# Three real products for four in the 128-point complex stages of a spectral and MLP kernel

## The chip, the cores and the metric

The kernel runs on one core of a Trainium2 chip. The metric is the device time of one execution in microseconds (us). Before the change it is 1355.37 us, the median of three runs (1354.95 to 1356.36).

The engines are named as in the profile: PE is TensorE, with PEld its weight loads; DVE is VectorE, ACT is ScalarE, POOL is GpSimd, SP is SyncE.

## The reference

A gated sum of two branches, and its gradients for eight of the inputs:

```python
def A(x, w_r, w_i):                      # spectral branch, x is (1, 2048, 1024)
    X = rfft2(x.astype(float32))
    return irfft2(X * (w_r + 1j * w_i), s=(S, D)).astype(bfloat16)

def B(x, w1, b1, w2, b2):                # MLP branch, F = 3584
    h = x @ w1 + b1
    return relu(h) ** 2 @ w2 + b2

g = sigmoid((x * gate_w).sum(-1, keepdims=True))
out = g * A(x, w_r, w_i) + (1 - g) * B(B_x, w1, b1, w2, b2)
# outputs: out, and the gradients with respect to x, w_r, w_i, w1, b1, w2, b2 and gate_w for grad_out
```

The kernel takes the second transform of 2048 points in the S direction as 16 x 128. The 16-point part and the part along D are done in an earlier stage. What is left for each of 16 residues k is a complex 128-point transform with twiddles, that is a product with a 128x128 complex matrix, cos and sin of which lie in `amat` (forward) and `apmat` (inverse). It is done for two transforms T: the input x (T = 0) and the gradient (T = 1).

## The kernel before

The large products of the MLP (forward, gradients of w1 and w2, gradient of x) are six groups of 896 matmuls of 128x512 in bf16. The spectral work is woven between them: the generator `spectra` is advanced at a fixed rate while `mlp_grads` yields. The program's builder then orders the instructions of each engine.

The stages of this study are in `fft_mid`, which runs beside the gradients of w2 and w1. One step m handles the two residues `pair(m)`, so that m goes from 0 to 7, and j = 0, 1 are the two residues of a pair:

```python
        for m in range(S2 // 2):
            z, am, ap, w = nxt
            if m + 1 < S2 // 2:
                nxt = inputs(m + 1)                      # loads for the next step
            xs = []
            for T in range(2):
                xs.append(spectrum(fb, T, m, z[:, T], am))   # forward, below
                yield
            real_columns(fb, m, z, am, xs, sgn)          # columns l = 0 and 512: tiny matmuls sp
            ...
            for T in range(2):                           # y = X * w, or X * conj(w)
                ...
                V(out=t1_[:, :, :, 0:W1], in0=X, in1=wr, op=ALU.mult)
                V(out=t2_[:, :, :, 0:W1], in0=X, in1=wi, op=ALU.mult)
                V(out=y[:, T, :, 0, 0:W1], ...)
                V(out=y[:, T, :, 1, 0:W1], ...)
                yield
            back(fb, m, y, ap)                           # inverse, below
            yield
            ...                                          # gradients of w: t1_, t2_, gs on VectorE
            nc.scalar.mul(out=gw[:, :, :, 0:W1], in_=gs[:, :, :, 0:W1], mul=GS)
            ...
            yield
```

The forward stage. `V` is a VectorE `tensor_tensor`, `mm` a matmul. A `px` tile is two PSUM banks, real and imaginary part, 512 columns each; there are two such tiles (`ps2`), which `pv` uses too:

```python
    def spectrum(fb, T, m, z, mats):
        if m:
            pm = fb.tile([P, 4, 4, P], FDT, name="pm", tag="pm")
            R, I = zg(z[:, 0]), zg(z[:, 1])[:, ::-1]
            V(out=pm[:, 2:0:-1], in0=R, in1=I, op=ALU.add)
            V(out=pm[:, 0::3], in0=R, in1=I, op=ALU.subtract)
            main = [(pm[:, 0], pm[:, 1]), (pm[:, 2], pm[:, 3])]
        else:
            ...
        x = fb.tile([P, 2, 2, LW], FDT, name=f"x{T}", tag=f"x{T}")
        for j in range(2):
            re, im = main[j]
            C, Sn, N = (mats[:, j, a, :] for a in range(3))      # cos, sin, -sin
            px = fps.tile([P, 2, H], FP32, name="px", tag="ps2", bufs=2)
            mm(px[:, 0, :], lhsT=C, rhs=re, start=True, stop=False)
            mm(px[:, 1, :], lhsT=C, rhs=im, start=True, stop=False)
            mm(px[:, 0, :], lhsT=Sn, rhs=im, start=False, stop=True)
            mm(px[:, 1, :], lhsT=N, rhs=re, start=False, stop=True)
            (nc.scalar.copy if j == 0 else nc.vector.tensor_copy)(
                out=x[:, j, :, 0:H].rearrange("p c (i g) -> p c i g", g=4), in_=px[:].rearrange("p c (g i) -> p c i g", g=4)
            )
        return x
```

The inverse stage `back` does the same four matmuls for `pv[:, 0]` and `pv[:, 1]` out of `y`, with `apmat`, for both T and both j, and copies `pv` to the fp16 tile `v` (ScalarE for j = 0, VectorE for j = 1). Then VectorE forms `pc` out of `v`, and GpSimd issues its store.

Another pair of PSUM buffers, one bank each (tag `tr`), serves the tiny products `sp` and `si` of the two single columns, the transposes and the column sums `prow`. The small inputs of `sp` and `si` are formed on GpSimd (`ed`, `e`).

Of the kernel before, what the change touches and what calls it, by code (L numbers as in the profile page):

```python
# [10 lines left out]
P = 128  # L11
BF16 = mybir.dt.bfloat16
FP16 = mybir.dt.float16
FP32 = mybir.dt.float32
# [3 lines left out]
FDT = FP16  # L18
# [25 lines left out]
def build_consts(g: Geo):  # L44


    S, D, S2 = g.S, g.D, g.S2
    tp = 2.0 * np.pi
    Q = D // 4
    c = {}  # L50
    c["identb"] = np.eye(P, dtype=np.float32).astype(ml_dtypes.bfloat16)
    q = np.arange(P)
    t, pl = q // 8, q % 8
    same = (pl[:, None] == pl[None, :]).astype(np.float64)

    cc = np.arange(16)
    k2 = np.where(cc <= 8, cc, cc - 8)
    ang = tp * ((np.arange(16)[:, None] * k2[None, :]) % 16) / 16
    kf = np.where(cc[None, :] <= 8, np.cos(ang), -np.sin(ang))
    c["kf"] = (kf[t][:, t] * same).astype(FDT_NP)  # L60
    ki = np.where(cc[None, :] <= 8, np.cos(ang), np.sin(ang)).T
    c["ki"] = (ki[t][:, t] * same).astype(FDT_NP)

    w = lambda l, d: tp * ((l[None, :] * d[:, None]) % D) / D
    l4, l42 = np.arange(0, D // 2 + 1, 4), np.arange(2, D // 2, 4)
    lo = np.concatenate([np.arange(1, D // 2, 4), np.arange(3, D // 2, 4)])
    d0, d1 = np.arange(P), np.arange(P, 2 * P)
    dz, dh = d0.copy(), d0.copy()
    dz[0], dh[0] = Q, P
    blk_n = np.concatenate([np.zeros((P, P + 1)), -np.sin(w(l4[1:-1], d0))], axis=1)  # L70
    blk_n[0, : P + 1] = np.cos(w(l4, np.array([P])))[0]
    parts = [
        blk_n, np.cos(w(l4, d0)), np.cos(w(l42, d0)), -np.sin(w(l42, dh)),
        np.cos(w(lo, d0)), np.cos(w(lo, d1)), -np.sin(w(lo, dz)), -np.sin(w(lo, d1)),
    ]
    c["cf"] = np.concatenate(parts, axis=1).astype(FDT_NP)

    v = lambda l, d: tp * ((l[:, None] * d[None, :]) % D) / D
    cof = lambda l: np.where((l == 0) | (l == 2 * Q), 1.0, 2.0)[:, None]
    dq = np.arange(Q)  # L80
    dzq = dq.copy()
    dzq[0] = Q
    m4, m42 = np.arange(0, D // 2, 4), np.arange(2, D // 2, 4)
    m1, m3 = np.arange(1, D // 2, 4), np.arange(3, D // 2, 4)
    da = np.arange(P + 1)
    ev = np.concatenate([np.zeros((P, P + 1)), -2.0 * np.sin(v(m4, da[1:-1]))], axis=1)
    ev[0] = 0.0
    ev[0, : P + 1] = np.cos(np.pi * da)
    parts = [
        ev, cof(m4) * np.cos(v(m4, da)), 2.0 * np.cos(v(m42, d0)), -2.0 * np.sin(v(m42, dh)),  # L90
        2.0 * np.cos(v(m1, dq)), 2.0 * np.cos(v(m3, dq)), -2.0 * np.sin(v(m1, dzq)), -2.0 * np.sin(v(m3, dzq)),
    ]
    c["ci"] = np.concatenate(parts, axis=1).astype(FDT_NP)

    pp = np.arange(P)
    A = np.zeros((P, S2, 3, P))
    B = np.zeros((P, S2, 3, P))
    for k in range(S2):
        th = tp * ((pp[:, None] * (k + S2 * pp[None, :])) % S) / S
        A[:, k, 0, :], A[:, k, 1, :], A[:, k, 2, :] = np.cos(th), np.sin(th), -np.sin(th)  # L100
        th = th.T
        B[:, k, 0, :], B[:, k, 1, :], B[:, k, 2, :] = np.cos(th), np.sin(th), -np.sin(th)
    c["amat"] = (A * XS).astype(FDT_NP)
    c["apmat"] = B.astype(FDT_NP)
    sg = np.ones((P, 2, 2, 2))
    sg[:, 1, 1, :] = -1.0
    c["sgn"] = sg.astype(np.float32)
    return c
# [19 lines left out]
def kernel(  # L128
# [172 lines left out]
    def zg(ap):  # L301
        return ap.rearrange("p (g c i) -> p c g i", g=4, c=2)
# [6 lines that stand above are left out]
            V(out=pm[:, 2:0:-1], in0=R, in1=I, op=ALU.add)  # L309
            V(out=pm[:, 0::3], in0=R, in1=I, op=ALU.subtract)  # L310
            main = [(pm[:, 0], pm[:, 1]), (pm[:, 2], pm[:, 3])]
        else:
            main = [(zg(z[:, j])[:, 0], zg(z[:, j])[:, 1]) for j in range(2)]
        x = fb.tile([P, 2, 2, LW], FDT, name=f"x{T}", tag=f"x{T}")
        for j in range(2):
            re, im = main[j]
            C, Sn, N = (mats[:, j, a, :] for a in range(3))
            px = fps.tile([P, 2, H], FP32, name="px", tag="ps2", bufs=2)
            mm(px[:, 0, :], lhsT=C, rhs=re, start=True, stop=False)
            mm(px[:, 1, :], lhsT=C, rhs=im, start=True, stop=False)  # L320
            mm(px[:, 0, :], lhsT=Sn, rhs=im, start=False, stop=True)
            mm(px[:, 1, :], lhsT=N, rhs=re, start=False, stop=True)  # L322
            (nc.scalar.copy if j == 0 else nc.vector.tensor_copy)(  # L323
                out=x[:, j, :, 0:H].rearrange("p c (i g) -> p c i g", g=4), in_=px[:].rearrange("p c (g i) -> p c i g", g=4)
            )
        return x

    def real_columns(fb, m, z, mats, xs, sgn):

        ed = fb.tile([P, 2, 2, 2, 2], FDT, name="ed", tag="ed", bufs=2)  # L330
        zc = z[:].rearrange("p t c l -> p c t l")[:, :, :, 0 : P + 1 : P]
        G = nc.gpsimd
        sp = tps.tile([P, 2, 2, 4], FP32, name="sp", tag="tr", bufs=2)
        if m:

            G.tensor_copy(out=ed[:, 0], in_=zc)
            G.tensor_copy(out=ed[:, 1, 0], in_=zc[:, 1])
            G.tensor_scalar(out=ed[:, 1, 1], in0=zc[:, 0], scalar1=-1.0, scalar2=None, op0=ALU.mult)
            src = [[ed[:, a].rearrange("p c t l -> p (c t l)") for a in range(2)]] * 2
        else:  # L340

            ed0 = fb.tile([P, 2, 3, 4], FDT, name="ed0", tag="ed0")
            G.memset(ed0[:], 0.0)
            G.tensor_copy(out=ed0[:, :, 0, :].rearrange("p j (t l) -> p j t l", t=2), in_=zc)
            G.tensor_scalar(
                out=ed0[:, :, 2, :].rearrange("p j (t l) -> p j t l", t=2), in0=zc, scalar1=-1.0, scalar2=None, op0=ALU.mult
            )
            src = [[ed0[:, j, a : a + 2, :].rearrange("p a b -> p (a b)") for a in range(2)] for j in range(2)]
        for j in range(2):
            C, Sn, N = (mats[:, j, a, :] for a in range(3))  # L350
            o = sp[:, j].rearrange("p c b -> p (c b)")
            mm(o, lhsT=C, rhs=src[j][0], start=True, stop=False, skip_group_check=True)
            mm(o, lhsT=(Sn if j == 0 else N), rhs=src[j][1], start=False, stop=True, skip_group_check=True)
        for T in range(2):
            V(out=xs[T][:, :, :, 0::H], in0=sp[:, :, :, 2 * T : 2 * T + 2], in1=sgn[:], op=ALU.mult)

    def back(fb, m, ys, mats):

        vs = []
        for T in range(2):  # L360
            y = ys[:, T]
            v = fb.tile([P, 2, 2, LW], FDT, name="v", tag="v", bufs=2)
            for j in range(2):
                C, Sn, N = (mats[:, j, a, :] for a in range(3))
                yr, yi = y[:, j, 0, :], y[:, j, 1, :]
                pv = fps.tile([P, 2, H], FP32, name="pv", tag="ps2", bufs=2)
                mm(pv[:, 0, :], lhsT=C, rhs=yr[:, 0:H], start=True, stop=False)
                mm(pv[:, 1, :], lhsT=C, rhs=yi[:, 0:H], start=True, stop=False)
                mm(pv[:, 1, :], lhsT=Sn, rhs=yr[:, 0:H], start=False, stop=True)
                mm(pv[:, 0, :], lhsT=N, rhs=yi[:, 0:H], start=False, stop=True)  # L370
                (nc.scalar.copy if j == 0 else nc.vector.tensor_copy)(out=v[:, j, :, 0:H], in_=pv[:])
            vs.append(v)

        G = nc.gpsimd
        e = fb.tile([P, 2, 2, 2], FDT, name="e1", tag="e1", bufs=2)
        yl = ys[:, :, :, :, H].rearrange("p t j c -> p j c t")
        G.tensor_scalar(out=e[:, :, 0, :], in0=yl[:, :, 1, :], scalar1=-1.0, scalar2=None, op0=ALU.mult)
        G.tensor_copy(out=e[:, :, 1, :], in_=yl[:, :, 0, :])
        sp = tps.tile([P, 2, 2, 2], FP32, name="si", tag="tr", bufs=2)
        for j in range(2):  # L380
            mm(sp[:, j], lhsT=mats[:, j, 0, :], rhs=yl[:, j], start=True, stop=False, skip_group_check=True)
            mm(sp[:, j], lhsT=mats[:, j, 1, :], rhs=e[:, j], start=False, stop=True, skip_group_check=True)
        for T in range(2):
            v = vs[T]
            nc.vector.tensor_copy(out=v[:, :, :, H], in_=sp[:, :, :, T])
# [663 lines left out]
```

## Time and profile before

| | |
|---|---|
| device time, median of 3 runs | 1355.37 us |
| span of the profiled execution | 1352.3 us |
| granted TensorE clock | 1.00 |
| first forward matmul `px` / last inverse matmul `pv` starts at | 478.7 / 809.5 us |
| `px` matmuls of 128x512 | 128 |
| `pv` matmuls of 128x512 | 128 |
| copies `x` out of `px`: ScalarE / VectorE | 16 / 16 |
| copies `v` out of `pv`: ScalarE / VectorE | 16 / 16 |

How to read it: the page gives for each engine its busy time, share of the span and count of instructions; then the span in 40 slices; then the chain of work that ended last, followed back from the end; then the groups of instructions, with the line, the engine, the operation, what is written and read, shapes and count, and after the bar the busy time in us and the mean of one in ns, and after a second bar the engine's idle time just before them and what ended it. Matmuls are pipelined, and their records overlap: how often one is issued is read from the starts in order of time. Some matmul records are missing from a trace.

### The profile page before, as it was taken

The page shows a single profiled execution, that of the slowest core. Times are in us where ns is not written, and L with a number is a line of the kernel's source. Part 1 is how long each engine was busy: PE and PEld are TensorE (multiplying, and loading weights), DVE is VectorE, ACT ScalarE, POOL GpSimd, SP SyncE. Part 2 cuts the span into 40 slices and gives each one's busy share as a digit, 9 for nine tenths or more (in the row PEclk, how much of TensorE's full clock was granted, in tenths as well). Part 3 has the DMA queues.
Part 4 walks back from the last instruction along what each step waited for, and adds up shares of the span by engine and source line. Part 5 has one row for each costly group of instructions (what it writes and reads, how often), then busy time and mean ns, then how long its engine had stood idle before and what let it go on. Part 6 is the DMA issues. An engine that isn't in the chain of part 4 may idle for free. (4 is left out here: it accounts for less than half of the span.)

```text
span 1352.3 us, 18733 instructions
## 1 busy us (share of the span) xinstructions
PE 1325.9 (98%) x7036; PEld 643.2 (48%) x7146; DVE 750.2 (55%) x1477; ACT 415.2 (31%) x626; POOL 293.2 (22%) x468
## 2 busy tenths in 40 slices
PE   7999999999999999999999999999999999999998
PEld 5654444444444444444444444555545444444443
DVE  7966667666565673556444552323855675642222
ACT  6854555555433313223132233343212100000000
POOL 0222223222322243443332221211101000000000
PEclk9999999999999999999999999999999999999999
DMA  8558778786778978889686448766888764653530
GB/s 284 184 179 252 254 232 258 246 251 225 228 234 242 287 220 194 219 196 235 183 186 190 113 139 245 237 225 215 234 227 232 180 195 132 190 168 94 155 101 24
DMA packets 217092, 273.31 MB, mean 202 GB/s; under 512 B 16988, under 2 KB 152170, under 8 KB 217002
## 3 DMA queue, kind: packets, MB, share of 16 engines
q1 hardware_dynamic: 181306, 153.84, 42.9%
q0 software_dynamic: 35696, 118.27, 27.3%
q8 instruction: 56, 0.92, 0.3%
q14 instruction: 34, 0.28, 0.1%
HBM read 147.25 MB, written 118.51 MB: 197 GB/s over the span
## 5 line engine op out<-in xcount | busy, mean ns | idle before, releaser
L602 PE MATMUL ph<-xT,w1g 128*128 128x512 bf16 x866 | 214.0, 381 | 4.0 <-ACT rT L604 1.7
L612 PE MATMUL pd<-dbT,w2T 128*128 128x512 bf16 x879 | 210.6, 379 | 2.6 <-DVE w2T L634 0.7
L823 PE MATMUL pw<-grd,res 128*128 128x512 bf16 x896 | 200.2, 379 | 0.0
L889 PE MATMUL acc<-w,hblk 128*128 128x512 bf16 x873 | 196.1, 379 | 2.7 <-DVE bGo L891 1.5
L806 PE MATMUL pw<-dbn,grp 128*128 128x512 bf16 x874 | 195.6, 379 | 0.8
L931 PE MATMUL accg<-w1Tr,hblk 128*128 128x512 bf16 x878 | 192.8, 379 | 0.9
L931 PEld LDWEIGHTS <-hblk 128*128 128x128 bf16 x896 | 87.6, 98 | 106.3 <-issue 0.9
L612 PEld LDWEIGHTS <-w2T 128*128 128x128 bf16 x896 | 87.2, 98 | 104.7 <-issue 1.5
L806 PEld LDWEIGHTS <-grp 128*128 128x128 bf16 x896 | 86.9, 98 | 104.2 <-issue 0.9
L889 PEld LDWEIGHTS <-hblk 128*128 128x128 bf16 x896 | 87.0, 98 | 101.1 <-issue 1.7
L602 PEld LDWEIGHTS <-w1g 128*128 128x128 bf16 x896 | 86.8, 98 | 100.0 <-issue 2.8
L823 PEld LDWEIGHTS <-res 128*128 128x128 bf16 x896 | 86.7, 98 | 98.7
L604 ACT ACTIVATE rT<-ph,b1col 128x512 bf16<-128x512 f32 x112 | 77.0, 688 | 144.9 <-PE ph L602 135.2
L616 DVE SCALAR_TENSOR_TENSOR dhT<-pd,rT 128x512 bf16<-128x512 f32 x112 | 75.2, 671 | 65.9 <-PE pd L612 57.3
L810 ACT CAST wo<-pw 128x512 bf16<-128x512 f32 x56 | 32.8, 586 | 161.1 <-PE pw L806 125.1
L936 DVE TENSOR_TENSOR gxo<-accg,g 128x512 bf16<-128x512 f32 x32 | 22.1, 691 | 107.9 <-PE accg L931 102.0
L721 DVE STREAM_TRANSPOSE stg<-h2T 128x512 int32<-128x512 int32 x56 | 39.8, 711 | 73.7 <-ACT h2T L605 73.7
L323 DVE CAST x<-px 128x1024 f16<-128x1024 f32 x16 | 19.6, 1224 | 105.1 <-PE px L322 105.1
L828 ACT CAST wo<-pw 128x512 bf16<-128x512 f32 x56 | 32.9, 587 | 132.0 <-PE pw L823 125.7
L818 POOL DMA_DIRECT2D out_dram<-wo x112 | 56.6, 518 | 72.6 <-ACT wo L810 65.0
L605 ACT ACTIVATE h2T<-rT 128x512 bf16<-128x512 bf16 x112 | 70.6, 630 | 3.1
L728 DVE STREAM_TRANSPOSE stgd<-dhT 128x1024 bf16<-128x1024 bf16 x56 | 69.3, 1239 | 1.3
(175 smaller groups left out, 1423.8 us busy)
## 6 DMA issues: line engine op xcount, KB each, us to landing
h2T_scr<-h2T POOLq DMA_DIRECT2D x28, 512.0 KB, 4.6
h_scr<-stg POOLq DMA_DIRECT2D x28, 512.0 KB, 6.9
dhT_scr<-dhT POOLq DMA_DIRECT2D x28, 512.0 KB, 7.7
dh_scr<-stgd POOLq DMA_DIRECT2D x28, 512.0 KB, 6.6
grp<-h_scr SPq DMA_DIRECT2D x112, 128.0 KB
grd<-dh_scr SPq DMA_DIRECT2D x112, 128.0 KB
hblk<-h2T_scr SPq DMA_DIRECT2D x8, 1792.0 KB
hblk<-dhT_scr SPq DMA_DIRECT2D x8, 1792.0 KB
```

Source lines behind the costliest of these rows:

```text
L602: mm(ph[:], lhsT=w1g[:, dc, fc % 2 * P : (fc % 2 + 1) * P], rhs=xT[:, dc, ss], start=(dc == 0), stop=(dc == DC - 1))
L604: nc.scalar.activation(rT[:], ph[:], ACT.Relu, bias=b1col[:, fc : fc + 1])
L605: nc.scalar.activation(h2T, rT[:], ACT.Square)
L612: mm(pd[:], lhsT=w_[:, ec // 2, ec % 2 :: 2], rhs=dbT[:, ec, ss], start=(ec == 0), stop=(ec == DC - 1),)
L616: return STT(out=dhT, in0=pd[:], scalar=2.0, in1=rT[:], op0=ALU.mult, op1=ALU.mult, accum_out=gb1part[:, fc, sb : sb + 1],)
L721: nc.vector.transpose(out=stg[:, :, c, :], in_=h2T[:, c, :].bitcast(I32).rearrange("p (b i) -> p b i", i=32))
L728: nc.vector.transpose(out=stg[:, :, :, c, :].rearrange("p b k i -> p k b i"), in_=dhT[:, c, :].rearrange("p (k b i) -> p k b i", b=4, i=32),)
L806: mm(pw[:], lhsT=cur[:, t // 2, 2 * fb_ * P + t % 2 : 2 * (fb_ + 1) * P : 2], rhs=dbn[:, t, hf * H : (hf + 1) * H], start=(t == 0), stop=( ...
L818: st(out=dst[q], in_=wo[32 * q : 32 * (q + 1), :])
L823: mm(pw[:], lhsT=xr[t][:, d_ * P : (d_ + 1) * P], rhs=cur[:, t], start=(t == 0), stop=(t == NT - 1),)
L889: mm(acc[:], lhsT=cur[:, fc, t2::2], rhs=w2[:, fc, cs], start=(fc == 0), stop=(fc == FC - 1))
L931: mm(acc[:], lhsT=cur[:, fc, t2::2], rhs=w1T[:, fc, 2 * hf : 2 * hf + 2, :], start=(fc == 0), stop=(fc == FC - 1),)
```

## The change

A complex product (C, S) with (re, im) needs the real part C·re + S·im and the imaginary part C·im - S·re, four real matrix products. They can be had from three: with the common product k = C·(re + im), the real part is k + (S - C)·im and the imaginary part is k - (C + S)·re. The matrices S - C and -C - S are constants and take the places of S and -S in `amat` and `apmat`. The sum re + im is one VectorE addition. The common product belongs to both parts, so it goes to a PSUM tile of its own, is copied to SBUF by ScalarE, and is added to the two others by VectorE as they are moved from PSUM. The change is there to do fewer matmuls.

```diff
@@ build_consts
-        A[:, k, 0, :], A[:, k, 1, :], A[:, k, 2, :] = np.cos(th), np.sin(th), -np.sin(th)
+        A[:, k, 0, :], A[:, k, 1, :], A[:, k, 2, :] = np.cos(th), np.sin(th) - np.cos(th), -np.cos(th) - np.sin(th)
... (B, for apmat, likewise)
@@ spectrum
+            re_, im_ = pm[:, 0::2], pm[:, 1::2]
...
+        sums = fb.tile([P, 2, 4, P], FDT, name="sums", tag="sums", bufs=2)
+        V(out=sums[:], in0=re_, in1=im_, op=ALU.add)
...
-            C, Sn, N = (mats[:, j, a, :] for a in range(3))
             px = fps.tile([P, 2, H], FP32, name="px", tag="ps2", bufs=2)
-            mm(px[:, 0, :], lhsT=C, rhs=re, start=True, stop=False)
-            mm(px[:, 1, :], lhsT=C, rhs=im, start=True, stop=False)
-            mm(px[:, 0, :], lhsT=Sn, rhs=im, start=False, stop=True)
-            mm(px[:, 1, :], lhsT=N, rhs=re, start=False, stop=True)
-            (nc.scalar.copy if j == 0 else nc.vector.tensor_copy)(
-                out=x[:, j, :, 0:H].rearrange("p c (i g) -> p c i g", g=4), in_=px[:].rearrange("p c (g i) -> p c i g", g=4)
+            ps = tps.tile([P, H], FP32, name="pxs", tag="tr", bufs=2)
+            mm(px[:, 0, :], lhsT=mats[:, j, 1, :], rhs=im, start=True, stop=True)
+            mm(px[:, 1, :], lhsT=mats[:, j, 2, :], rhs=re, start=True, stop=True)
+            mm(ps[:], lhsT=mats[:, j, 0, :], rhs=sums[:, j], start=True, stop=True)
+            common = fb.tile([P, H], FP32, name="common", tag="common", bufs=2)
+            nc.scalar.copy(out=common[:], in_=ps[:])
+            by_l = lambda ap: ap.rearrange("p c (g i) -> p c i g", g=4)
+            V(
+                out=x[:, j, :, 0:H].rearrange("p c (i g) -> p c i g", g=4), in0=by_l(px[:]),
+                in1=by_l(common[:].rearrange("p (o l) -> p o l", o=1)).to_broadcast([P, 2, P, 4]), op=ALU.add,
             )
@@ back
+            sums = fb.tile([P, 2, H], FDT, name="ysums", tag="sums", bufs=2)
+            V(out=sums[:], in0=y[:, :, 0, 0:H], in1=y[:, :, 1, 0:H], op=ALU.add)
             for j in range(2):
... (two matmuls to pv, one to pvs in a "tr" buffer, ScalarE copy to common, as above)
+                V(
+                    out=v[:, j, :, 0:H], in0=pv[:],
+                    in1=common[:].rearrange("p (o l) -> p o l", o=1).to_broadcast([P, 2, H]), op=ALU.add,
+                )
@@ real_columns, for m > 0
-            G.tensor_copy(out=ed[:, 0], in_=zc)
+            G.tensor_tensor(out=ed[:, 0, 0], in0=zc[:, 0], in1=zc[:, 1], op=ALU.add)
+            G.tensor_tensor(out=ed[:, 0, 1], in0=zc[:, 1], in1=zc[:, 0], op=ALU.subtract)
@@ back, single columns
+        G.tensor_tensor(out=e[:, :, 1], in0=e[:, :, 0], in1=yl, op=ALU.add)
```

The single columns use the same matrices, so their small inputs on GpSimd are formed anew: since S·b = (S - C)·b + C·b, what multiplied C gets the other operand added. The numbers of their matmuls stay as they were.

More of the change, by code (lines that the diff above doesn't have):

```diff
@@ L99, in build_consts @@
         th = tp * ((pp[:, None] * (k + S2 * pp[None, :])) % S) / S
-        A[:, k, 0, :], A[:, k, 1, :], A[:, k, 2, :] = np.cos(th), np.sin(th), -np.sin(th)
+        A[:, k, 0, :], A[:, k, 1, :], A[:, k, 2, :] = np.cos(th), np.sin(th) - np.cos(th), -np.cos(th) - np.sin(th)
         th = th.T
-        B[:, k, 0, :], B[:, k, 1, :], B[:, k, 2, :] = np.cos(th), np.sin(th), -np.sin(th)
+        B[:, k, 0, :], B[:, k, 1, :], B[:, k, 2, :] = np.cos(th), np.sin(th) - np.cos(th), -np.cos(th) - np.sin(th)
     c["amat"] = (A * XS).astype(FDT_NP)
@@ L311, in spectrum @@
             main = [(pm[:, 0], pm[:, 1]), (pm[:, 2], pm[:, 3])]
+            re_, im_ = pm[:, 0::2], pm[:, 1::2]
         else:
             main = [(zg(z[:, j])[:, 0], zg(z[:, j])[:, 1]) for j in range(2)]
+            re_, im_ = (z.rearrange("p j (g c i) -> p c j g i", g=4, c=2)[:, c] for c in range(2))
+        sums = fb.tile([P, 2, 4, P], FDT, name="sums", tag="sums", bufs=2)
+        V(out=sums[:], in0=re_, in1=im_, op=ALU.add)
         x = fb.tile([P, 2, 2, LW], FDT, name=f"x{T}", tag=f"x{T}")
@@ L340, in real_columns @@
         else:
-            ed0 = fb.tile([P, 2, 3, 4], FDT, name="ed0", tag="ed0")
+            ed0 = fb.tile([P, 2, 4, 4], FDT, name="ed0", tag="ed0")
             G.memset(ed0[:], 0.0)
             G.tensor_copy(out=ed0[:, :, 0, :].rearrange("p j (t l) -> p j t l", t=2), in_=zc)
[L345 to L348, printed above, removed]
+            for a in (1, 3):
+                G.tensor_scalar(
+                    out=ed0[:, :, a, :].rearrange("p j (t l) -> p j t l", t=2), in0=zc, scalar1=-1.0, scalar2=None, op0=ALU.mult
+                )
+            src = [[ed0[:, j, a : a + 2, :].rearrange("p a b -> p (a b)") for a in (0, 2)] for j in range(2)]
         for j in range(2):
-            C, Sn, N = (mats[:, j, a, :] for a in range(3))
             o = sp[:, j].rearrange("p c b -> p (c b)")
-            mm(o, lhsT=C, rhs=src[j][0], start=True, stop=False, skip_group_check=True)
-            mm(o, lhsT=(Sn if j == 0 else N), rhs=src[j][1], start=False, stop=True, skip_group_check=True)
+            mm(o, lhsT=mats[:, j, 0, :], rhs=src[j][0], start=True, stop=False, skip_group_check=True)
+            mm(o, lhsT=mats[:, j, 1 + j, :], rhs=src[j][1], start=False, stop=True, skip_group_check=True)
         for T in range(2):
@@ L362, in back @@
             v = fb.tile([P, 2, 2, LW], FDT, name="v", tag="v", bufs=2)
+            sums = fb.tile([P, 2, H], FDT, name="ysums", tag="sums", bufs=2)
+            V(out=sums[:], in0=y[:, :, 0, 0:H], in1=y[:, :, 1, 0:H], op=ALU.add)
             for j in range(2):
-                C, Sn, N = (mats[:, j, a, :] for a in range(3))
-                yr, yi = y[:, j, 0, :], y[:, j, 1, :]
                 pv = fps.tile([P, 2, H], FP32, name="pv", tag="ps2", bufs=2)
-                mm(pv[:, 0, :], lhsT=C, rhs=yr[:, 0:H], start=True, stop=False)
@@ L368, in back @@
[L368 to L371, printed above, removed]
+                ps = tps.tile([P, H], FP32, name="pvs", tag="tr", bufs=2)
+                mm(pv[:, 0, :], lhsT=mats[:, j, 2, :], rhs=y[:, j, 1, 0:H], start=True, stop=True)
@@ new lines, in back @@
+                mm(pv[:, 1, :], lhsT=mats[:, j, 1, :], rhs=y[:, j, 0, 0:H], start=True, stop=True)
+                mm(ps[:], lhsT=mats[:, j, 0, :], rhs=sums[:, j, :], start=True, stop=True)
+                common = fb.tile([P, H], FP32, name="common", tag="common", bufs=2)
+                nc.scalar.copy(out=common[:], in_=ps[:])
+                V(
+                    out=v[:, j, :, 0:H], in0=pv[:],
+                    in1=common[:].rearrange("p (o l) -> p o l", o=1).to_broadcast([P, 2, H]), op=ALU.add,
+                )
@@ L372, in back @@
             vs.append(v)
         G = nc.gpsimd
-        e = fb.tile([P, 2, 2, 2], FDT, name="e1", tag="e1", bufs=2)
+        e = fb.tile([P, 2, 2, 2, 2], FDT, name="e1", tag="e1", bufs=2)
         yl = ys[:, :, :, :, H].rearrange("p t j c -> p j c t")
-        G.tensor_scalar(out=e[:, :, 0, :], in0=yl[:, :, 1, :], scalar1=-1.0, scalar2=None, op0=ALU.mult)
-        G.tensor_copy(out=e[:, :, 1, :], in_=yl[:, :, 0, :])
+        G.tensor_scalar(out=e[:, :, 0, 0, :], in0=yl[:, :, 1, :], scalar1=-1.0, scalar2=None, op0=ALU.mult)
@@ L379, in back @@
+        G.tensor_copy(out=e[:, :, 0, 1, :], in_=yl[:, :, 0, :])
+        G.tensor_tensor(out=e[:, :, 1], in0=e[:, :, 0], in1=yl, op=ALU.add)
         sp = tps.tile([P, 2, 2, 2], FP32, name="si", tag="tr", bufs=2)
         for j in range(2):
-            mm(sp[:, j], lhsT=mats[:, j, 0, :], rhs=yl[:, j], start=True, stop=False, skip_group_check=True)
-            mm(sp[:, j], lhsT=mats[:, j, 1, :], rhs=e[:, j], start=False, stop=True, skip_group_check=True)
+            mm(sp[:, j], lhsT=mats[:, j, 0, :], rhs=e[:, j, 1], start=True, stop=False, skip_group_check=True)
+            mm(sp[:, j], lhsT=mats[:, j, 1, :], rhs=e[:, j, 0], start=False, stop=True, skip_group_check=True)
```

## The prediction

> **What bounds the kernel now.** I read the page from the top: busy shares, chain, groups; then the busy time by stretches, and last the order of time on each engine around one of the changed stages.
>
> The first part of the page and the chain (part 4):
>
> ```profile
> PE 1325.9 (98%) x7036; PEld 643.2 (48%) x7146; DVE 750.2 (55%) x1477; ACT 415.2 (31%) x626; POOL 293.2 (22%) x468
> ...
> PE 22%; issue 0%; DVE 0%
> ```
>
> TensorE is busy 98% of the span, and the chain that ended last holds TensorE alone, as far back as it could be followed. So a matmul that goes away should shorten the run, unless TensorE then waits.
>
> The busy time by stretches; the columns are the stretch, its length, the busy time and count of each engine, the granted clock, the DMA share:
>
> ```profile
> 478.00:815.00 337.00, 335.49 (x1588) 152.28 (x1607) 178.44 (x266) 93.90 (x120) 116.03 (x206) 1.00 0.75 187
> 815.00:1352.00 537.00, 527.19 (x2718) 252.77 (x2756) 247.16 (x578) 79.78 (x93) 51.23 (x93) 1.00 0.62 178
> ```
>
> All changed stages lie in the first of the two (their first matmul starts at 478.7 us, their last at 809). There TensorE idles 337.0 - 335.5 = 1.5 us, VectorE is busy 53% and ScalarE 28%. Nothing there waits on TensorE's account now; I ask what will.
>
> The groups, kept apart by shape (mean ns of one after the bar):
>
> ```profile
> L367 PE MATMUL pv<-y,apmat 128*128 128x512 f16 x32 | 12.1, 378 | 0.7 <-DVE v L371 0.2
> L371 DVE CAST v<-pv 128x1024 f16<-128x1024 f32 x16 | 19.6, 1222 | 9.0 <-PE pv L370 9.0
> L371 ACT CAST v<-pv 128x1024 f16<-128x1024 f32 x16 | 16.1, 1009 | 5.9 <-PE pv L370 5.9
> L388 DVE TENSOR_TENSOR pc<-v 128x1024 f16<-128x1024 f16 x14 | 9.7, 690 | 3.3 <-ACT v L371 2.9
> L936 DVE TENSOR_TENSOR gxo<-accg,g 128x512 bf16<-128x512 f32 x32 | 22.1, 691 | 107.9 <-PE accg L931 102.0
> L810 ACT CAST wo<-pw 128x512 bf16<-128x512 f32 x56 | 32.8, 586 | 161.1 <-PE pw L806 125.1
> ```
>
> These are my price list. Last, TensorE, VectorE and ScalarE in order of time round the inverse stage of m = 2 (start, duration):
>
> ```profile
> 581.96 0.17 PE L352 MATMUL sp<-ed,amat 128*128 128x8 f16 x1
> ...
> 592.42 0.38 PE L367 MATMUL pv<-y,apmat 128*128 128x512 f16 x1
> 592.64 0.38 PE L368 MATMUL pv<-y,apmat 128*128 128x512 f16 x1
> ```
> ```profile
> 582.53 1.23 DVE L432 TENSOR_TENSOR t<-x,w 128x2052 f16<-128x2052 f16 x1
> ...
> 592.98 0.69 DVE L447 TENSOR_TENSOR gs<-t 128x1026 f16<-128x1026 f16 x1
> 594.36 1.23 DVE L371 CAST v<-pv 128x1024 f16<-128x1024 f32 x1 [0.69 <-PE pv L370]
> ```
> ```profile
> 592.67 0.59 ACT L810 CAST wo<-pw 128x512 bf16<-128x512 f32 x1 [2.91 <-PE pw L806]
> 593.70 1.92 ACT L449 ACTIVATE gw<-gs 128x2052 bf16<-128x2052 f16 x1 [0.45 <-DVE gs L447]
> ```
>
> Two things: a matmul is issued every 0.216 us although its record lasts 0.38; and VectorE works without a pause from the `sp` matmul to the end of `gs`, at 593.67, which is 1.25 us after `pv` has begun. The slack of VectorE at this point is already used up.
>
> [...] So a removed matmul is worth 0.216 us and not 0.378. [...] 1024 elements take 1222 ns from PSUM and 690 ns from fp16 SBUF. [...]
>
> **The change, part by part.**
>
> *Removed from TensorE.* There are 8 steps m, 2 transforms T, 2 blocks j, forward and inverse: 64 blocks, each with three matmuls of 128x512 in place of four. 64 x 0.216 = 13.8 us. The tiny matmuls (`sp`, `si`) stay 32 of each kind.
>
> *VectorE.* Before: 32 casts of 1024 from PSUM at 1.22 (the other 32 are ScalarE's). After: 64 adds of 1024 with one PSUM and one fp32 operand. L936 is that form at 512 elements, 691 ns, against 690 ns for 1024 in fp16[...]. Added: 32 x 1.22 = 39 us. Then 32 sums of 1024 in fp16 at 0.69 = 22 us. Together 61 us in this stretch: 178 + 61 = 239 of about 330, 73%. VectorE doesn't become the bound by throughput.
>
> *ScalarE.* Away: 32 x 1.01 = 32 us. Added: 64 casts of 512 at 0.586 = 37.5 us. Even.
>
> *GpSimd.* One small addition more for `ed` and one for `e1` in each step, 0.2 to 1.2 us each going by the small copies at L337, L377. `e` is ready some 1.0 us before `pv` begins in the trace (590.15 + 1.25 = 591.4), and its matmul comes later than before; hidden.
>
> *New latency.* A `px`/`pv` buffer used to come free one cast (1.0 or 1.2 us, on two engines side by side) after its last matmul. Now: third matmul, ScalarE copy 0.59, then VectorE add 1.22, and all adds on one engine. There are still two such buffers, and two for the common product.
>
> I laid the order of instructions of the built program, engine by engine, against these durations. In the inverse stage TensorE issues: two `pv` matmuls and one common for T0 j0, the same for j1 (6), one filler of the large product, common of T1 j0, two fillers, common of T1 j1, one filler, then `pv` of T1 j0. So `pv` of T1 j0 is reached after 12 x 0.216 = 2.59 us and needs the add of T0 j0 done.
>
> - Steps with 48 fillers between `sp` and `pv`, which are m = 1, 2, 3, 7. The built order puts the two `ysums` (0.61 each from issue to issue, and a short wait: 1.3) and the `gs` group ahead of the first add. `gs` ends at 1.25 + 1.3 = 2.55 after `pv` begins. The add of T0 j0 then runs 2.6 to 3.85. Stall: 3.87 - 2.59 = 1.28 us. The second add ends at 4.97; TensorE reaches its buffer at 3.87 + 0.43 + 4 x 0.216 = 5.16, no wait. 4 x 1.28 = 5.1 us.
> - m = 0 has the other small matmuls between and another order: about 0.4 us.
> - m = 4, 5, 6 have 64 fillers: `gs` is done before `pv`, the add waits only for the copy (0.9 to 1.5 us), runs to 2.7: 0.15 us each, 0.45.
> - Forward stages: mostly 32 fillers (6.9 us) lie between T0 and T1, and VectorE's chain there (pm 0.68, two adds 1.15 each, pm, sums) is done in about 5.7 us. Only m = 3 has 16 (3.5 us): 0.5 us. There ScalarE also stood behind an output store before (its copy of `px` came 3 us late); as it now feeds VectorE, that may cost 2 to 3 us. I put 1.7 for m = 3 in all.
>
> Stalls: 5.1 + 0.4 + 0.45 + 1.7 = 7.7 us. Net: 13.8 - 7.7 = 6.1 us. 1355.4 - 6.1 = 1349.3 us. Nothing after this stretch changes on TensorE, so the gain should reach the end.
>
> **The rivals.**
>
> *All hidden.* The fillers cover every eviction and the whole 13.8 us arrive: 1341.6. For it: the 1.5 us of idle now, 73% VectorE load, fillers placed around the waits. Against it: VectorE has no pause before `pv` at m = 2, and it gets 1.3 us more there.
>
> *VectorE's chain sets the pace.* An early delay isn't made up within a step, so that `sums` of the next forward stage is late too, stalls at the forward and the inverse stages sum to the saving or more: 1355 to 1362. For it: [...] `gw` (1.92 us on ScalarE, waiting for `gs`) stands between the commons of T0 and T1 in m = 1, 2, 3, 7. Against it: VectorE idles some 8.6 us per step before the first `px` cast and 6.2 before the second, and the added work is 7.7 us per step, so each step should catch up.
>
> *A buffer shared with others.* The common products use the two PSUM buffers that `sp`, `si` and `prow` use. If a late copy held these, TensorE would wait at `si` or `sp`: perhaps 0.5 us a step, 4 us in all, 1353. The built order puts `si` late, which speaks against much of it.
>
> **Range and chances.** No stall gives 1341.6, my sum 1349.3, twice my stalls 1357. The low side is held by TensorE's arithmetic. I take 1343 to 1356. Faster by over 2% would need under 1328.3, twice the matmul time removed: 0.01. Slower by over 2%, above 1382.5, would need 40 us of stalls, 5 a step: 0.02. Within 2%: 0.97.
>
> **What would show each step.** The added time on VectorE: 64 adds near 1.22 us, 32 sums near 0.69. TensorE's busy count down by 64 matmuls; its idle time in the stretch up from 1.5 to about 9 us, put down to the VectorE add at the `pv` matmul of T1, 1.3 us each in m = 1, 2, 3, 7 and next to nothing in m = 4, 5, 6. The stretch from first `px` to last `pv` shorter by about 6 us, the time before and after unchanged. I am wrong if the adds take longer than 1.3 us because of their strided output or the broadcast operand (then every stall grows by the difference), if the waits at `px` exceed those at `pv`, or if the stretch behind it moves by more than 2 us.

## The result, and the profile after

The changed kernel takes 1352.74 us (median of 4 runs, 1350.59 to 1353.24) against 1355.16 us for the kernel before on the same chip: a ratio of 0.9979 (0.9961 to 0.9996). The gain is 2.4 us where 6.1 was predicted. A second measurement, ten runs, is among the experiments below: 1351.38 us, 0.9977 (0.9968 to 0.9986). The experiments ran on three chips (1 to 4, 5 to 8 and 9 to 11), each beside the kernel before, with medians of 1354.46, 1354.68 and 1354.87 us; a ratio is to the kernel before on the same chip.

From the page of the changed kernel, first the busy shares, then the chain that ended last:

```profile
PE 1322.1 (98%) x7082; PEld 637.1 (47%) x7082; DVE 824.3 (61%) x1541; ACT 418.4 (31%) x658; POOL 299.3 (22%) x484
...
PE 20%; DMA 1%; DVE 1%; SPq 0%; issue 0%; DVEq 0%
PE accg L946 14%; PE acc L904 6%; DMA go<-in_grad_out_dram 1%; DVE af L898 0%; PE prow L762 0%; DVE ot L905 0%; DVE junk L906 0%; DVE junk L894 0%; SPq L914 0%; DVE gxo L951 0%; SPq L861 0%; DVE ev L496 0%; DVE ev L498 0%; DVE ev L499 0%; DVE ev L500 0%
```

Before, this chain was TensorE alone. Now a load (`go`, the output gradient) and some VectorE work on it stand in it, in the MLP's output stage (`acc`, the last group of matmuls but one), which the change doesn't touch.

The busy time by stretches (stretch, length, busy time and count of PE, PEld, DVE, ACT, POOL, granted clock, DMA share, GB/s); the first again runs from the first `px` to past the last `pv`:

```profile
478.00:812.00 334.00, 324.99 (x1546) 145.52 (x1545) 253.16 (x330) 97.24 (x153) 122.47 (x222) 1.00 0.75 188
812.00:1351.00 539.00, 530.54 (x2756) 253.03 (x2754) 246.39 (x578) 79.74 (x93) 51.22 (x94) 1.00 0.61 178
```

VectorE has 253 us in the first, not 239. The tiles say why (shortest/median/longest in ns, then the first and the last start):

```profile
L330 DVE TENSOR_TENSOR x<-px,common x32: 1890/1922/1935, 482.3 to 786.0; 128x1024 f16<-128x1024 f32 x32
...
L382 DVE TENSOR_TENSOR v<-pv,common x32: 1204/1214/1225, 509.6 to 807.6; 128x1024 f16<-128x1024 f32 x32
```

The inverse adds (L382) take the 1.21 us expected of both; the forward ones (L330) take 1.92. That is 32 x 0.70 = 22 us of work more than priced; the busy time, in which records that overlap count once, shows 14 of them.

Who made TensorE wait (total us, times, longest):

```profile
PE pvs L379 <- ACT common L381: 3.6, 3, 1.2
PE pv L377 <- DVE v L382: 2.8, 4, 0.7
PE acc L904 <- DVE bGo L906: 2.4, 1, 2.4
...
PE px L325 <- DVE pm L311: 1.6, 2, 1.2
```

Idle time here begins only at the end of the last record, which lasts 0.38 us while matmuls are issued every 0.216: each pause is some 0.16 us longer than the view says. Below, a pause in the first stretch is the distance of two starts less 0.216; for the output stage the idle time of the view is given as it stands.

**Where the time went.** Two marks divide the run: the first `acc` matmul and the first `accg` matmul of the stage after it. In the profiled run of the kernel before, first `px` to first `acc` takes 456.8 us (478.7 to 935.5) and `acc` to `accg` 217.4. In the changed kernel:

```profile
L904 PE MATMUL acc<-w,hblk x896: 376/379/634, 931.7 to 1151.9; 128*128 128x512 bf16 x180
```

This is 453.1 us (931.7 - 478.6); `accg` begins at 1152.1, 220.4 us later. So two questions: why the first stretch gains 3.7 us and not 6.1, and why the output stage gives 3.0 of them back in this run.

**The pauses in the first stretch.** In m = 3, a step with 48 fillers, TensorE (start, duration):

```profile
631.45 0.38 PE L377 MATMUL pv<-y,apmat 128*128 128x512 f16 x1
...
634.89 0.38 PE L377 MATMUL pv<-y,apmat 128*128 128x512 f16 x1 [0.69 <-DVE v L382]
```

and VectorE:

```profile
633.01 0.69 DVE L462 TENSOR_TENSOR gs<-t 128x1026 f16<-128x1026 f16 x1
633.62 2.34 DVE L382 TENSOR_TENSOR v<-pv,common 128x1024 f16<-128x1024 f32 x2
```

The adds start when `gs` ends, 2.17 us after `pv` began, and T1's `pv` is held until the first add is done: 3.44 - 2.59 = 0.85 us. In m = 4, with 64 fillers, it is another engine. TensorE and ScalarE:

```profile
676.76 0.38 PE L377 MATMUL pv<-y,apmat 128*128 128x512 f16 x1
...
679.68 0.38 PE L379 MATMUL pvs<-ysums,apmat 128*128 128x512 f16 x1 [1.24 <-ACT common L381]
```
```profile
676.76 1.92 ACT L464 ACTIVATE gw<-gs 128x2052 bf16<-128x2052 f16 x1 [2.62 <-DVE gs L462]
678.58 0.57 ACT L825 CAST wo<-pw 128x512 bf16<-128x512 f32 x1
679.04 1.08 ACT L381 COPY common<-pvs 128x512 f32<-128x512 f32 x2
```

`gs` ends just as `pv` begins, ScalarE starts `gw` at once, and the copies of both common products stand behind it: T1's third matmul finds its PSUM buffer, one of the two with the tag `tr`, full for 1.41 us. No VectorE add is waited for here.

### The profile page after: what moved, and what is told of

Read it like the earlier page. It is cut to its first block, busy times and chain, and to the rows that moved or that the text cites. A ratio compares the mean times of both kernels' runs of the same rounds, so it can differ in the third digit from the quotient of the medians.

```text
span 1351.5 us, 18838 instructions
## 1 busy us (share of the span) xinstructions
PE 1322.1 (98%) x7082; PEld 637.1 (47%) x7082; DVE 824.3 (61%) x1541; ACT 418.4 (31%) x658; POOL 299.3 (22%) x484
## 5 line engine op out<-in xcount | busy, mean ns | idle before, releaser
L617 PE MATMUL ph<-xT,w1g 128*128 128x512 bf16 x896 | 218.5, 381 | 2.0 <-ACT rT L619 1.7
L904 PE MATMUL acc<-w,hblk 128*128 128x512 bf16 x896 | 199.8, 381 | 2.4 <-DVE bGo L906 2.4
L821 PE MATMUL pw<-dbn,grp 128*128 128x512 bf16 x896 | 200.4, 379 | 0.0
L496 DVE TENSOR_TENSOR ev<-e 128x256 f16<-128x256 f16 x32 | 9.3, 289 | 93.5 <-ACT e L493 93.4
```

The source lines that it names most:

```text
L617: mm(ph[:], lhsT=w1g[:, dc, fc % 2 * P : (fc % 2 + 1) * P], rhs=xT[:, dc, ss], start=(dc == 0), stop=(dc == DC - 1))
L821: mm(pw[:], lhsT=cur[:, t // 2, 2 * fb_ * P + t % 2 : 2 * (fb_ + 1) * P : 2], rhs=dbn[:, t, hf * H : (hf + 1) * H], start=(t == 0), stop=( ...
L904: mm(acc[:], lhsT=cur[:, fc, t2::2], rhs=w2[:, fc, cs], start=(fc == 0), stop=(fc == FC - 1))
```

## The experiments

Theory A: the stalls in the 128-point stages are queues (VectorE's `gs` and ScalarE's `gw` ahead of the evictions), made worse by forward adds that read the fp32 common product with a stride; the output stage's loss is a separate thing, a load that an earlier TensorE waits for. Rival B: VectorE as a whole sets the pace. Rival C: what is gained ahead of a late load is lost whatever the adds cost.

**1. The common product laid out contiguously.** Forward only, ScalarE writes it in the order in which the add reads it:

```diff
-            nc.scalar.copy(out=common[:], in_=ps[:])
+            nc.scalar.copy(out=common[:].rearrange("p (i g) -> p g i", g=4), in_=ps[:].rearrange("p (g i) -> p g i", g=4))
-                in1=by_l(common[:].rearrange("p (o l) -> p o l", o=1)).to_broadcast([P, 2, P, 4]), op=ALU.add,
+                in1=common[:].rearrange("p (o i g) -> p o i g", o=1, g=4).to_broadcast([P, 2, P, 4]), op=ALU.add,
```

> Edit: ScalarE writes the forward common product in the order in which VectorE reads it, so that VectorE's second operand is contiguous; nothing else. Theory A (the 512-byte stride of the fp32 second operand costs the forward add 0.70 us each): the 32 forward adds fall from 1.92 to about 1.22 us, ScalarE's copy stays near 0.59, TensorE's pauses at px/pxs of m = 3, 4 (2.7 us) fall below 1, those at pvs of m = 4, 5, 6 (1.4 each) shrink too because VectorE's chain starts earlier; first px to first acc shrinks from 453.2 to about 449.5 us, time about 1349. Rival (broadcast or the strided output makes them slow, or the strided PSUM operand): adds stay at 1.92, time stays at 1352.7.

Measured: 1348.0 us, 0.9949 (0.9937 to 0.9962); `px` to `acc` 447.8 us. The tiles of this kernel:

```profile
L328 ACT COPY common<-pxs x32: 1074/1122/1174, 479.9 to 778.7; 128x512 f32<-128x512 f32 x32
L330 DVE TENSOR_TENSOR x<-px,common x32: 1211/1215/1226, 482.2 to 780.1; 128x1024 f16<-128x1024 f32 x32
```

The adds fall to 1.22 us with output, PSUM operand and broadcast as they were, so the stride of the second operand was the whole of the 0.70 us. Not expected: the cost moves partly to ScalarE, whose copy rises from 0.585 to 1.12 us. The pauses of m = 4, 5, 6 fall from 1.36 to 1.41 to between 0.25 and 0.29, although `gw` is where it was; those of m = 1, 2, 3, 7 stay at 0.85 to 0.89.

**2 and 3. Forward stage alone, inverse stage alone.**

```diff
@@ forward only: back and apmat as in the kernel before
-                mm(pv[:, 0, :], lhsT=mats[:, j, 2, :], rhs=y[:, j, 1, 0:H], start=True, stop=True)
... (to the add)
+                mm(pv[:, 0, :], lhsT=C, rhs=yr[:, 0:H], start=True, stop=False)
... (the four matmuls and the copy to v of before)
@@ inverse only: spectrum, real_columns and amat as in the kernel before, back as changed
```

> Three products in the forward stage alone, the inverse stage with four as before. Theory (the pauses belong to the stage that has the change): 32 matmuls or 6.9 us less on TensorE, new pauses only at px/pxs (about 3.3 us in the changed kernel), so first px to first acc about 453 to 454 us and a time of about 1351.5 to 1353. Rival (all VectorE load is one pool and any part of it pushes the rest): pauses at pv too, and no gain against before.

> Three products in the inverse stage alone, the forward stage with four as before. Theory: 6.9 us less on TensorE; pauses at pv of T1 of 0.9 us in m = 1, 2, 3, 7 stay; those at pvs in m = 4, 5, 6 (1.4 us in the changed kernel) are smaller, near 0.5, as the slow forward adds no longer delay VectorE; first px to first acc about 453 us, time about 1351 to 1352.5. Rival (the pauses at pvs come from ScalarE's gw alone, whatever VectorE did before): they stay at 1.4.

Measured: forward only 1355.86 us, 1.0010 (1.0003 to 1.0016), slower with 32 matmuls less; inverse only 1351.79, 0.9978 (0.9968 to 0.9987), as much as the whole change. These are the signs that the expectation gave to its rival (pauses at `pv` too, no gain), not those of its theory. Most of the loss is in step m = 3; ScalarE, then TensorE:

```profile
612.32 0.58 ACT L819 CAST wo<-pw 128x512 bf16<-128x512 f32 x1 [6.62 <-DMA out_dram<-wo]
612.80 1.08 ACT L328 COPY common<-pxs 128x512 f32<-128x512 f32 x2
```
```profile
615.38 0.39 PE L324 MATMUL px<-pm,amat 128*128 128x512 f16 x1 [2.09 <-DVE x L330]
617.78 0.38 PE L325 MATMUL px<-pm,amat 128*128 128x512 f16 x1 [2.02 <-DVE pm L311]
```

A `wo` cast that waits for the store of an earlier `wo` holds up the copies behind it, these the adds, and these TensorE: two pauses of 2.26 and 2.19 us. TensorE then had half its clock: the mean granted clock is 0.95 from 615 to 619 us and 0.62 from 619 to 623, which makes 3.4 us at 0.50. That the store is behind these two pauses is read from the waits; no run took it away. The inverse stage is that of before here, and yet m = 4, 5, 6 pause (0.89 to 0.92), where the kernel before had next to nothing: `gs` comes late behind the slow forward adds, and `gw` and `wo` then stand on ScalarE ahead of its cast of `v`. Inverse only has the pauses of m = 1, 2, 3, 7 (0.91 to 0.97), which are thus the inverse stage's own, but 0.32 in m = 4, 5, 6. There `gs` ends 1.13 us ahead of `pv`; in the changed kernel 0.04. The 1.4 us come from both together: forward adds that let the step begin late, and `gw` in front.

**4 and 5. A third buffer for the `go` load,** in the kernel before and in the changed kernel:

```diff
-                go = wb.tile([P, D], BF16, name="go3", tag="go3", bufs=2)
+                go = wb.tile([P, D], BF16, name="go3", tag="go3", bufs=3)
... (xo, which uses the same buffers, likewise)
```

> The kernel before, with three instead of two buffers for the go rows of the output stage, so that their loads are issued ahead of the large loads there. It measures the wait near 1080 us by itself. Theory (the wait for go near 1080 us, 1.5 us of TensorE idle in the kernel before, is a load issued too late): the wait goes, the time falls by 1 to 1.5 us to about 1354. Rival (the memory traffic itself is the limit there): the wait stays or moves to another load, time 1355.

> The changed kernel with three buffers for the go rows, as in e4. Theory B (the changed kernel reaches the load of go near 1075 us earlier than the load can follow, waits 2.5 us in place of 1.5, and TensorE's clock is then halved for 3.4 us, which costs 1.7): the wait goes, no half-clock stretch stands near 1080 us, and the time falls by 3 to 4 us, to a ratio of about 0.995 to 0.996 of before. Rival (the end of the gain is lost to the stages of the change alone): only the 1.65 us that e4 won, ratio about 0.9967.

First what there is to be removed. The changed kernel's TensorE, VectorE and SyncE's DMA queue in the output stage:

```profile
1077.87 23.43 PE L904 MATMUL acc<-w,hblk 128*128 128x512 bf16 x100 [2.45 <-DVE bGo L906]
```
```profile
1073.82 1.23 DVE L894 CUSTOM_DVE_ANT_0 junk<-af,go 128x1024 bf16<-128x1024 f32 x1 [12.51 <-DMA go<-in_grad_out_dram]
```
```profile
1045.83 12.91 SPq L914 DMA_DIRECT2D w1Tr<-w1T_scr  x4
...
1059.38 9.91 SPq L890 DMA_DIRECT2D go<-in_grad_out_dram  x1
```

`go` is issued at 1059.38 us, behind the weights in the queue (12.91 us), and lands 14.4 us later. VectorE then works for 4 us (1073.82 to 1077.87) before `acc` is emptied, and TensorE stands for 2.45 of them. The kernel before has the same pause at 1080.42, but of 1.46. Its `go`, issued at 1062.93, is first used here:

```profile
1076.37 1.22 DVE L879 CUSTOM_DVE_ANT_0 junk<-af,go 128x1024 bf16<-128x1024 f32 x1 [11.51 <-DMA go<-in_grad_out_dram]
```

That is 13.4 us after the issue. So the changed kernel issues the load 3.55 us sooner, as much as TensorE comes sooner (the matmul ahead of the pause starts at 1075.04 for 1078.59), but the load takes 1.0 us longer, and by that the pause grows. With two buffers it takes 13.3 to 13.5 us in the kernel before and in experiments 2 and 3, and 14.4 to 14.9 in the changed kernel and in experiments 1, 6, 7 and 11; why is not shown. And then two stretches of the changed kernel (columns as above), before and after the end of the pause:

```profile
1075.61:1079.02 3.41, 1.15 (x6) 0.56 (x6) 3.32 (x8) 0.00 (x0) 0.25 (x1) 1.00 0.79 225
1079.02:1082.44 3.42, 3.42 (x10) 1.24 (x9) 3.42 (x8) 0.00 (x0) 0.29 (x1) 0.50 1.21 290
```

From 1079.02 to 1082.44 us TensorE has half its clock: 0.50 x 3.4 = 1.7 us are lost. Longer pause (1.0) and half clock (1.7) make 2.7 of the 3.0 us.

Measured: the kernel before with the third buffer 1352.81 us, 0.9989 (0.9983 to 0.9996); the changed kernel with it 1348.07, 0.9949 (0.9935 to 0.9962). `acc` to `accg` is 215.8 us in both. The same place in the changed kernel now:

```profile
1072.00:1076.00 4.00, 4.00 (x20) 1.78 (x19) 3.98 (x10) 0.00 (x0) 0.00 (x0) 1.00 0.18 47
```

No idle time, full clock. With the load out of the way the change is worth 1352.81 - 1348.07 = 4.7 us, or 5.4 by the two ratios, as these two ran on different chips. So its loss behind the stretch was this load's. Rival C holds for that part alone: experiment 1 meets the same late load, yet of the 9.0 us that its `px` to `acc` is shorter than before it gives back only 2.8 in the output stage.

**6. `gw` behind the common copies,** an order and nothing else (`after(a, b, ...)` puts a behind b in the order of their engine; `later` only keeps b at hand):

```diff
-                nc.scalar.copy(out=common[:], in_=ps[:])
+                later["common"] = nc.scalar.copy(out=common[:], in_=ps[:])
-            nc.scalar.mul(out=gw[:, :, :, 0:W1], in_=gs[:, :, :, 0:W1], mul=GS)
+            gw_ = nc.scalar.mul(out=gw[:, :, :, 0:W1], in_=gs[:, :, :, 0:W1], mul=GS)
+            after(gw_, later["common"], mybir.DependencyClass.NoSync)
```

> The changed kernel, where ScalarE's scaling gw is ordered behind the last inverse common copy of its step; nothing else. Theory C (gw, 1.92 us, stands ahead of the first common copy in m = 4, 5, 6 and holds it): TensorE's pauses at pvs there, 1.4 us each and 0.2 behind, fall below 0.4; the pauses of 0.9 at pv in m = 1, 2, 3, 7 stay; first px to first acc 453.2 to about 449.5 us. Rival (the add on VectorE is the late one, whatever ScalarE does): pauses in m = 4, 5, 6 stay above 1.

Measured: 1349.24 us, 0.9958 (0.9946 to 0.9971); `px` to `acc` 450.8. ScalarE in m = 4 of this kernel:

```profile
678.00 0.59 ACT L826 CAST wo<-pw 128x512 bf16<-128x512 f32 x1 [2.82 <-PE pw L822]
678.65 1.23 ACT L381 COPY common<-pvs 128x512 f32<-128x512 f32 x2
...
682.20 1.92 ACT L464 ACTIVATE gw<-gs 128x2052 bf16<-128x2052 f16 x1
```

The copies come first, and no pause of m = 4, 5, 6 is over 0.16 us, with the slow forward adds unchanged. Part of the gain is lost again in m = 3, where the pause at `px` grew from 1.32 to 2.19 us, with half clock behind it; there a `wo` cast that had waited 4.51 us for a store stood ahead of the copies. (The granted clock is 0.71 from 612 to 616 us and 0.86 from 616 to 620.)

**7. And `gs` behind the adds of T0:** as 6, and

```diff
+            after(V(out=gs[:, :, 0, 0:W1], ...), later["vadd", 0, 1], mybir.DependencyClass.NoSync)
... (the second gs operation likewise; "vadd" holds the inverse adds)
```

> As e6, and the two gs operations of VectorE are ordered behind the adds of T0. Theory D (gs, 1.3 us, stands ahead of the first add in m = 1, 2, 3, 7): TensorE's pauses at pv there fall from 0.9 to about 0.2; first px to first acc about 447 us. Rival (VectorE is short of time in these steps, and what is moved back delays the next forward stage): new pauses at px or pxs of about the same sum, 449.5 us stays.

Measured: 1345.07 us, 0.9928 (0.9916 to 0.9941); `px` to `acc` 445.4. The pauses of m = 1, 2, 3, 7 fall to 0.15. VectorE does the same work in another order, so it was the order that cost them, and rival B falls. In m = 3, 1.34 + 0.30 us are left in the forward stage, and in the output stage a pause of 2.84 us with half clock.

**8. Everything together:** the edits of 1 and 7, and the third `go` buffer of 4.

> Everything together: the common product written in the order of reading (e1), gw and gs ordered behind (e7), three buffers for go (e5). Theory (the four causes are separate and add up): pauses between px and acc near those of before, 2 to 3 us, first px to first acc about 443 to 444 us, time about 1340 us, ratio 0.988 to 0.990. Rival (they cover one another, or the loads of the output stage take the gain back): ratio 0.992 or above.

Measured: 1341.3 us (1340.32 to 1342.0), 0.9899 (0.9885 to 0.9912), the best version, 1.0% faster than the kernel before and clearly faster than the changed one. `px` to `acc` takes 444.0 us, `acc` to `accg` 215.8. Its first stretch:

```profile
478.00:800.00 322.00, 320.44 (x1515) 144.24 (x1532) 229.47 (x324) 110.86 (x151) 119.76 (x218) 1.00 0.75 192
```

TensorE idles 1.6 us, as before the change, and of the 13.8 us of matmuls 456.8 - 444.0 = 12.8 arrive.

**9 to 11. Is the output stage's loss there every time?** The changed kernel again, without an edit; the kernel before with one `go` buffer in place of two (`bufs=1`, both tiles); and version 8 with its two `go` buffers (`bufs=2`).

> The changed kernel once more, unchanged, beside the kernel before on one chip, to have its time from more runs. 1352 to 1353 us, ratio 0.998, with one half-clock stretch of 3.4 us in some of the runs.

> The kernel before with one buffer in place of two for the go rows (and the xo rows, which share the tag), so that many loads of the output stage come late; it has none of the change. It asks whether a pause of TensorE by itself brings the half clock. Theory: there are several pauses at acc, and those over about 2.4 us are followed by a stretch of half clock, those under 1.6 us are not; the time grows by the pauses and 1.7 us for each such stretch, 1360 to 1420 us. Rival (the half clock belongs to something in the changed stages): pauses of over 2.4 us and the clock at 1.00 after them.

> As e8, but with the two go buffers of before. Theory (the better the changed stages, the more the late load of go takes back): first px to first acc about 443.5 to 444 us as in e8, but a pause of 2.5 to 3 us near 1070 us and a half-clock stretch in most runs; 3 to 5 us slower than e8's 1341.3, about 1345. Rival (the load follows the earlier start): 1.65 us slower, 1343.

Measured. The changed kernel: 1351.38 us (1349.79 to 1353.48). Its profiled run, the fastest, has a pause of 2.90 us in the output stage and no half clock behind it: `acc` to `accg` 218.8, which is the 217.4 of before and the 1.4 us by which the pause grew. Five of its ten runs lie between 1349.8 and 1350.8 and four between 1352.8 and 1353.5. The mean granted clock is 1.000 in four of the lower five, which leaves no room for a stretch of half clock (3.4 us of it would make 0.999), and 0.999 in all the upper ones, which agrees with one. The two groups lie some 3 us apart, more than the 1.7 us of one stretch; the rest is open.

The kernel before with one buffer: 1371.87 us (2 runs), 1.0129 (1.0103 to 1.0154). Nothing of the change is in it, and it has pauses of 6.79 and 2.23 us on this same wait, each with half clock behind it (after the second, one `acc` matmul takes 0.55 us for 0.38). A third stretch of half clock, in which eight `pui` matmuls from 1046.74 us take 1.36 us in place of 0.91, comes after three waits of 1.16 to 1.59 us at `pki` and `pui`. TensorE after the longest pause:

```profile
1082.57 26.98 PE L889 MATMUL acc<-w,hblk 128*128 128x512 bf16 x110 [6.79 <-DVE bGo L891]
```

The granted clock is 0.50 between 1082 and 1086 us. So the pause and the half clock come here without the change. Version 8 with two buffers: 1343.28 us, 0.9919 (0.9906 to 0.9933), with a pause of 2.44 us and half clock in the output stage. In the medians the third buffer is worth 2.0 us there (2.7 by the ratios), less than I expected and near the rival's figure: the load is issued sooner here too, at 1050.45 us, and takes 14.4 us as in the changed kernel. Between the two profiled runs `acc` to `accg` differs by 4.3 (220.1 and 215.8).

## Why the prediction was off, step by step

The time fell inside the range, and TensorE's bound, the price of a matmul and the cause of the waits of m = 1, 2, 3, 7 were right. The gain was 2.4 to 3.5 us by the two measurements, not 6.1. Three steps failed.

| pauses of TensorE, us | predicted | measured |
|---|---|---|
| m = 1, 2, 3, 7: T1's `pv` behind the add | 5.1 | 3.5 (0.89, 0.85, 0.85, 0.90) |
| m = 4, 5, 6 | 0.45 | 4.7 (1.59, 1.54, 1.55) |
| m = 0 | 0.4 | 0.7 |
| forward, m = 3 and 4 | 1.7 | 2.7 (1.62, 1.10) |
| sum | 7.7 | 11.6 |

- **Every add of 1024 at the cast's 1.22 us: failed for the forward adds.** They take 1.92 us. The price was my estimate, from a cast that has no second operand. I named it as the way to be wrong, but suspected the output and the broadcast; experiment 1 shows the stride of the second fp32 operand. It made VectorE late in the forward stages (m = 3, and m = 4 together with a `wo` cast that waited 6.13 us for a store), and experiment 3 shows that without it m = 4, 5, 6 pause 0.32 + 0.18 us. Removing it alone brought about 4 us (a ratio of 0.9949 for 0.9979). Inverse adds (1.21) and sums (0.69) were priced right. The 1.7 us put down for m = 3 nearly came (1.62), but by luck: they were meant for a wait behind a store, and in the profiled run the copies of m = 3 have none ahead of them; the two slow adds made the pause.
- **"`gs` is done before `pv`, the add waits only for the copy": failed for m = 4, 5, 6.** I followed VectorE's order there and not ScalarE's, where `gw` and `wo` stand ahead of the copies. This is the largest miss, 4.7 us for 0.45. Either cure works alone: `gw` behind the copies (experiment 6) or, nearly, faster forward stages (1, 3). The rival on VectorE's pace had named `gw`, but for the other four steps. The rival on shared buffers had named the two `tr` buffers and 4 us, but at `si` or `sp`; TensorE waits for them at `pvs`.
- **"Nothing after this stretch changes on TensorE, so the gain should reach the end": failed.** The instructions are the same, but their times against a load aren't. TensorE arrives 3.55 us sooner, `go` only 2.55, and the pause grows from 1.46 to 2.45 us, with 1.7 us of half clock behind it; in the second profiled run it is 2.90 us, without half clock. With a third buffer the gain passes (experiment 5).
- **m = 1, 2, 3, 7: mechanism right, size too large.** `gs` ends 2.17 us after `pv` begins, where I had 2.55, so that the pause is 0.87 us on average and not 1.28. Experiment 7 confirms the mechanism.
- **"All hidden" nearly came true,** once the orders and the stride were mended: 1341.6 was that rival's figure, and experiment 8 gives 1341.3 with the third buffer, which by itself is worth 1.65 us (experiment 4); with two buffers the time is 1343.28 (experiment 11).

The sum of it: 13.8 us removed; pauses of 11.6 us in the stretch, where the kernel before had about 1.3 at its `pv` matmuls (0.37 and three of 0.30; missing matmul records may hide more), so about 3.5 us should be left, and 3.7 are. The idle time of the windows went from 1.5 to 9.0 us, just as I wrote, but by luck, for the gain is smaller: most pauses lose 0.16 us each in that view, and pauses under 0.16 us don't show at all. My 7.7 was issue time and should not have been held against it.

## What to carry to other kernels

When an eviction moves to another engine, read both engines' queues at every step, not at one: an unrelated 1.92 us activation ahead of a 0.59 us copy cost TensorE 1.4 us, and an order alone won it back. Price an elementwise operation by a row with the same strides in every operand, not only the same size and memories. And before counting on a gain at the end, look for the next place where the faster engine meets a load that doesn't come sooner by as much; one more buffer there was worth as much here as the change (a ratio of 0.9949 for 0.9979).

## What the runs showed of the hardware

- **A strided fp32 operand in SBUF.** 1024 elements out of PSUM plus fp32 from SBUF: 1.92 us where neighbours in the add's order lie 512 bytes apart (changed kernel), 1.22 where they are contiguous (experiment 1). The PSUM operand has the same step in both and costs nothing for it: the inverse adds, with a contiguous PSUM operand, take 1.21. ScalarE's copy of 512 elements takes 1.12 us when it writes with a step of 16 bytes (experiment 1), 0.585 without. No other step was tried, and why a step costs this is not shown.
- **Half clock after short pauses.** By the idle time of the view, pauses of 2.45 us (changed kernel), 2.44 (version 8 with two buffers), 2.53 (experiment 1), 2.84 (experiment 7) and even 2.02 (experiment 6, m = 3) were followed by half clock; 2.65 (experiment 6, output stage) and 2.90 (changed kernel again) were not. The granted clock is 0.50 from 1079.02 to 1082.44 us in the changed kernel; means over 4 us are 0.81 and 0.77 behind the pause of 2.53 (1070 to 1078 us) and 1.00 behind those of 2.65 (1076 to 1080 us) and 2.90 (1074 to 1082 us). In experiment 7 and in version 8 with two buffers the sign is the longest `acc` matmul, 0.631 and 0.634 us for a median of 0.379; it is 0.379 in experiment 6. So in these runs the length of a pause does not tell whether half clock follows; what does is not shown, as no experiment moved a pause by itself. The loss, 1.7 us, is half of the 3.4 us that the stretch lasts in the changed kernel.
